# A check of the sums behind the last eviction, with a second path behind a branch

## The chip, the cores and the metric

The kernel runs on one core of one Trainium2 chip. A core has five engines with queues of their own (PE multiplies matrices, DVE and ACT work on vectors, POOL does side work, SP issues transfers) and 16 DMA engines that move data between the device memory and the core. The metric is the device time of one execution in microseconds. A profiled execution also has a span, from the first to the last instruction of the core, which is a little shorter than its time.

## The reference

A gated recurrence runs over time for each batch and channel; its output is mixed by 32 slots of 8 experts, with a softmax over all tokens (columns) on the way in and a softmax over the slots (rows) on the way out.

```python
sig = 1.0 / (1.0 + np.exp(-f_logit))             # x, f_logit: 4 x 5056 x 256
f = lower_bound + (1.0 - lower_bound) * sig
for t in range(S):                                # S = 5056
    h = f[:, t] * h + (1.0 - f[:, t]) * x[:, t]
    y[:, t] = h
...
x = y.reshape(20224, 256)
logits = x @ phi                                  # 20224 x 32
d = np.exp(logits - logits.max(0)); d /= d.sum(0) + 1e-09
slot_input = d.T @ x                              # 32 x 256, 4 slots for each expert
for e in range(8):
    slot_out[e] = np.maximum(slot_input[e] @ w1[e], 0.0) @ w2[e]
c = np.exp(logits - logits.max(1)); c /= c.sum(1) + 1e-09
out = c @ slot_out
```

## The kernel before

*Stages.* The input is read once, in units of 512 time steps of one batch (n counts the units, g the groups of four batches, b the batch). For each unit ACT takes the sigmoid, POOL multiplies with x (u_t), PE turns both to channels on the partitions, ACT makes the decay, DVE scans along time (line 318), PE turns the result back and makes the logits, and ACT takes the exponential of the logits **without subtracting a maximum**: all exponentials stay on the chip in etall (32 slots of each of four batches on 128 partitions), with their sums over time in csum. After the last unit the small experts' stage runs on the weights loaded meanwhile, and gives slot_out. The last stage multiplies etall with slot_out, 128 rows at a time, scales each row by the reciprocal of its row sum, and stores the rows.

*The sums.* Row sums come from matmuls of etall with ones (row_sums) into rs_ps, and their reciprocals go to the tile rrow, one column for each block of 128 rows and each batch (lines 726 and 741); the last 64 time steps use left and only half of the last four columns. The column sums are reduced by DVE from csum to cs1 (line 628, one column on 128 partitions), which a matmul with rep2 adds up over the batches (cs_ps, line 659), and DVE takes the reciprocal (rcs, line 667).

*The last stage.* The pool osb has three buffers for output rows; the pool pout, opened in line 786 on the kernel's outermost stack of contexts, has the eight banks of PSUM. whole(i, b, ...) handles one batch by itself, couple(i, j) two batches at once: a matmul for each row of the block (line 813), then an eviction with the scale by ACT (line 818) or DVE (line 821), then the stores, 2048 KB each, issued by SP (line 833). The last calls are couple(i, j) over the full blocks, so the program's last work is three buffers of evictions and six stores. The tile base holds the identity matrix in its first 128 columns and other constants; its first 512 columns are reused as begun, for the first output rows.

*Order.* The instructions of each engine stand in the order of the calls (manual_schedule); waits between engines are set by the framework from the tiles that are read and written. At the end of the program a closing block (line 890 in the profile) lets SP wait for all transfers, after which all engines meet at a barrier. An opening block (line 879) fills four constants on POOL and lets all engines start by a barrier.

Of the kernel before, what the change touches and what calls it, by code (L numbers as in the profile page):

```python
# [9 lines left out]
F32 = mybir.dt.float32  # L10
BF16 = mybir.dt.bfloat16
AX = mybir.AxisListType
ALU = mybir.AluOpType
ACT = mybir.ActivationFunctionType
PSUM = bass.MemoryType.PSUM


@with_exitstack
def kernel(
# [10 lines left out]
    nc = tc.nc  # L30
    B, S, D = x.shape
    E = moe_w1.shape[0]
    F = moe_w1.shape[2]
    NS = moe_phi.shape[1]
    SPE = NS // E
    P = 128
    DC = D // P
    FC = F // P
    R = 4
    G = P * R  # L40
    n_grp = (S + G - 1) // G
# [27 lines left out]
    phi = consts.tile([P, DC, NS], BF16, name="phi")  # L69
    base = consts.tile([P, 2 * P + P // 2 + D], F32, name="base")  # L70
    ident_f = base[:, ds(0, P)]
    make_identity(nc, ident_f)
    ident = base[:, ds(P, P // 2)].bitcast(BF16)
    rep = base[:, ds(P + P // 2, P)].rearrange("p (b s) -> p b s", b=B)
# [3 lines left out]
    lbs = consts.tile([P, 4, DC], F32, name="lbs")  # L78
    omlb, nomlb = lbs[:, 0], lbs[:, 1]
    own = lbs[:, 2, ds(0, 1)]  # L80
# [42 lines left out]
    rrow = store.tile([P, n_grp * R, B], F32, name="rrow")  # L123
# [36 lines left out]

    psu = held.enter_context(tc.tile_pool(name="psu", bufs=2, space=PSUM))
    psp = held.enter_context(tc.tile_pool(name="psp", bufs=1, space=PSUM))
    ld = held.enter_context(tc.tile_pool(name="ld", bufs=3))
    with tc.tile_pool(name="sp2", bufs=3) as sp2, \
# [4 lines left out]
         tc.tile_pool(name="etok", bufs=2) as etok, \  # L169
         tc.tile_pool(name="ptp", bufs=1, space=PSUM) as ptp, \  # L170
         tc.tile_pool(name="plg", bufs=1, space=PSUM) as plg, \
         tc.tile_pool(name="pslot", bufs=1, space=PSUM) as pslot:

# [12 lines left out]
        xs, fs, sts, uts, pss, psus, hs, hps, hts, lgs, ets = ({} for _ in range(11))  # L186
# [402 lines left out]
        hid, wide = (ld.tile([P, 2, R, D], F32, name=i, tag="x_t") for i in ("hid", "wide"))  # L589
        hid = hid.rearrange("p u r d -> p (u r d)").bitcast(BF16)[:, ds(0, FC * E // 2 * NS)]  # L590
# [3 lines left out]
        hid = hid.rearrange("p (f e s) -> p f e s", f=FC, s=NS)  # L594
# [17 lines left out]
        for o in range(DC):  # L612
            nc.tensor.matmul(sin_ps[:, o], slot_v[:, o], rep[:, 0],
                             start=True, stop=True, skip_group_check=True)

    with tc.tile_pool(name="ew", bufs=1) as ew, \
         tc.tile_pool(name="pm", bufs=2, space=PSUM) as pm, \
         tc.tile_pool(name="pbig", bufs=1, space=PSUM) as pbig:
# [3 lines left out]
        sin = [ew.tile([P, NS], BF16, name=f"sin{o}") for o in range(DC)]  # L622
# [1 line left out]
        nc.scalar.activation(sin[1], sin_ps[:, 1], ACT.Copy, scale=omlb[:, ds(1, 1)])  # L624
        row_sums(8, 14)

        cs1 = ew.tile([P, 1], F32, name="cs1")
        nc.vector.tensor_reduce(cs1, csum, AX.X, ALU.add)


# [3 lines left out]
        for q in range(E // Q):  # L634
            hi = ew.tile([P, F], BF16, name=f"hi{q}")
            for k in range(2):
                hi_ps = (psu.tile([P, H], F32, name="hi_ps", tag="up") if q == 0 else
                         pbig.tile([P, H], F32, name="hi_ps", tag=f"hi_ps{k}"))
                for o in range(DC):
                    for j in range(Q):  # L640
                        nc.tensor.matmul(hi_ps[ds(j * NS, NS)], sin[o],
                                         w1_sb[q * Q + j][:, o, ds(k * H, H)],
                                         start=(o == 0), stop=(o == DC - 1),
                                         skip_group_check=True)
# [8 lines left out]
        for q in range(E // Q):  # L653
# [4 lines left out]
            if q == 0:  # L658
                nc.tensor.matmul(cs_ps, rep2, cs1, start=True, stop=True)
                src = ht_ps.rearrange("p f (j s) -> p f j s", s=NS)[:, :, :, ds(0, SPE)]  # L660
                src = bass.AP(tensor=src.tensor, offset=src.offset,
                              ap=[list(src.ap[0]), [P, FC], [NS + SPE, Q], [1, SPE]])
                dst = hid[:, :, :, ds(0, SPE)]
                dst = bass.AP(tensor=dst.tensor, offset=dst.offset,
                              ap=[list(dst.ap[0]), [Q * NS, FC], [NS + SPE, Q], [1, SPE]])
# [4 lines left out]
            for j in range(Q):  # L670
                s0 = (Q + j) * SPE
                src = ht_ps[:, :, ds(j * NS + s0, SPE)]
# [3 lines left out]
        top = ds((B - 1) * NS, NS)  # L676
# [9 lines left out]
        for e in range(Q):  # L686
            for fc in range(FC):
                nc.tensor.matmul(so4_ps[ds(fc % 4 * NS, NS), :], hid[:, fc, e],
                                 w2_sb[e][:, fc],
                                 start=(e == 0 and fc < 4),  # L690
                                 stop=(e == Q - 1 and fc >= FC - 4),
                                 skip_group_check=True)
# [14 lines left out]
        for j in range(Q):  # L707
            for fc in range(FC):
                if j == Q - 1 and fc == half:
# [5 lines left out]
                                 start=(j, fc) in ((0, 0), (Q - 1, half)),  # L715
                                 stop=j == Q - 1 and fc in (half - 1, FC - 1),
                                 skip_group_check=True)
# [3 lines left out]
            if j == 0:  # L721
                nc.tensor.matmul(so_ps, rep2, so4, start=False, stop=False,
                                 skip_group_check=True)
                for k in range(0, wide_r, wide_r // 4):
                    k = ds(k, wide_r // 4)
                    nc.vector.reciprocal(rrow[:, k], rs_ps[:, k])
                for i in range(0, half, 2):
                    g_ps = psu.tile([P, 2, DIR, P], F32, name="g_ps", tag="up")
                    for k in range(2):
                        nc.tensor.matmul(g_ps[:, k], hi_late[top, i + k], em[top],  # L730
                                         start=True, stop=True, skip_group_check=True)
# [5 lines left out]
            if j == 1:  # L737
                row_sums(25, n_grp * R)
                q = n_grp * R - 1
                k = ds(wide_r * B, (q - wide_r) * B + B // 2)  # L740
                nc.vector.reciprocal(rrow.rearrange("p q b -> p (q b)")[:, k],
                                     rs_ps.rearrange("p q b -> p (q b)")[:, k])
        for r in range(DIR):
            add(r, (FC - 2, FC - 1), False)
            nc.tensor.matmul(rows_ps[r], early[:, r], slot_pre,
                             start=False, stop=True, skip_group_check=True)
# [3 lines left out]
        for r in range(DIR):  # L750
            scale = rrow[:, r, ds(B - 1, 1)]
            if r == 0:
                nc.scalar.activation(begun[:, r], rows_ps[r], ACT.Copy, scale=scale)
            else:
# [3 lines left out]
            out=out[ds((B - 1) * S, P * wide_r)].rearrange(  # L758
                "(p r) d -> p r d", r=wide_r)[:, ds(0, DIR)], in_=begun)


    held.close()
    with tc.tile_pool(name="osb", bufs=3, reuse_waits="tile") as osb:

        def by_vector(ob, op, scale):
            nc.vector.tensor_tensor(ob, op, scale.broadcast_to(list(ob.shape)), ALU.mult)
# [15 lines left out]
        def rows_of(i, b):  # L782
            t0, n_r = blocks[i]
            return out[ds(b * S + t0, P * n_r)].rearrange("(p r) d -> p r d", r=n_r)

        pout = ctx.enter_context(tc.tile_pool(name="pout", bufs=8, space=PSUM, reuse_waits="tile"))

        def whole(i, b, pieces, ends):
            n_r = blocks[i][1]
# [71 lines left out]
        for i in range(end):  # L861
            for j in range(B // 2):
                if i or j < B // 2 - 1:
                    couple(i, j)


# [1 line left out]
_INS = ['x', 'f_logit', 'lower_bound', 'moe_phi', 'moe_w1', 'moe_w2']  # L868
# [26 lines left out]
```

## Time and profile before

| What | Value |
|---|---|
| median of three runs | 197.6 us (196.98 to 198.33) |
| profiled execution, its own time | 197.07 us |
| its span | 195.3 us |
| busy PE, DVE, ACT, POOL | 154.1, 146.5, 139.9, 103.6 us |
| moved by the DMA engines | 70.75 MB, 362 GB/s on the mean |
| share of the 16 DMA engines: SP's queue, POOL's queue, code | 76.8%, 21.6%, 0.4% |
| last eviction ends, last store's bytes end | 176.1 us, 193.0 us |

Busy time counts when an engine executes; a wait is put down to what ended last. The profile cuts the span into 40 slices and gives the busy share of each in tenths. Queries of the trace give single instructions: line, engine, operation, the tiles as output<-input, the shape, a count, and times in microseconds or, for single instructions in groups, nanoseconds (shortest/median/longest). A q behind an engine's name is its queue: instructions that wait, issue transfers or work on semaphores.

### The profile page before, as it was taken

How to read it: one execution, taken by the hardware profiler on the slowest of the kernel's cores; microseconds unless marked ns; L12 is line 12 of the kernel's file. 1: busy time of each engine (PE TensorE's matmuls, PEld its weight loads, DVE VectorE, ACT ScalarE, POOL GpSimd, SP SyncE). 2: the span in 40 equal slices, each digit the busy share in tenths (PEclk: the TensorE clock that was granted, in tenths of full speed). 3: DMA queues.
4: the chain of work that ended last, by engine and by line, in shares of the span. 5: the costliest groups of instructions: out<-in, count | busy, mean ns of one | idle time of the engine just before them, and what ended most of it. 6: DMA issues, size and time to landing. Idle time of an engine off the chain costs nothing.

```text
span 195.3 us, 3281 instructions
## 1 busy us (share of the span) xinstructions
PE 154.1 (79%) x1206; PEld 105.1 (54%) x1206; DVE 146.5 (75%) x191; ACT 139.9 (72%) x201; POOL 103.6 (53%) x80
## 2 busy tenths in 40 slices
PE   4758888999989979888997878999899999980000
PEld 4436666776767757666685756468675433220000
DVE  2679788899799999999999999534189798770000
ACT  3689698699789999999998595634279987770000
POOL 2589578874997789884979968284030000000000
PEclk9999999999999999999999999999997555555555
DMA  5999999999999999999999999999949999999995
GB/s 202 415 419 419 434 424 424 424 426 358 380 428 419 417 321 423 430 419 313 397 421 388 275 232 213 214 212 214 181 152 424 421 454 430 430 430 430 430 430 218
DMA packets 14145, 70.75 MB, mean 362 GB/s; under 512 B 1569, under 2 KB 2594, under 8 KB 10162
## 3 DMA queue, kind: packets, MB, share of 16 engines
q1 hardware_dynamic: 11504, 62.13, 76.8%
q0 software_dynamic: 2624, 8.42, 21.6%
q8 instruction: 9, 0.15, 0.3%
q14 instruction: 6, 0.05, 0.1%
q10 hardware_dynamic: 2, 0.00, 0.0%
HBM read 58.23 MB, written 20.71 MB: 404 GB/s over the span
## 4 chain that ended last, share of the span: by engine, by line
DMA 30%; PE 21%; DVE 17%; ACT 10%; issue 6%; POOL 5%; ACTq 0%; SPq 0%; POOLq 0%; DVEq 0%
DMA x_t<-in_x_dram 15%; DVE h L318 14%; PE op L813 9%; DMA w_t<-in_moe_w_dram 8%; DMA w_sb<-in_moe_w_dram 7%; POOL u_t L247 4%; ACT oc L818 4%; DVE ht L348 3%; PE hp L331 3%; PE up L272 2%; ACT a L300 2%; PE op L776 2%; PE sp L262 2%; ACT ob L770 1%; ACT s_t L236 1%
## 5 line engine op out<-in xcount | busy, mean ns | idle before, releaser
L247 POOL TENSOR_TENSOR u_t<-s_t,x_t 128x1024 bf16<-128x1024 bf16 (+1 forms) x39 | 82.4, 2128 | 22.1 <-ACT s_t L236 13.2
L318 DVE TENSOR_TENSOR_SCAN h<-a,h,up 128x512 bf16<-128x512 f32 (+1 forms) x72 | 86.7, 1252 | 4.6 <-PE up L272 3.3
L236 ACT ACTIVATE s_t<-f_t 128x2048 bf16<-128x2048 f32 (+2 forms) x23 | 38.3, 1669 | 7.4 <-DMA f_t<-in_f_logit_dram 5.2
L331 PE MATMUL hp<-base,h 128*128 128x128 f32 (+1 forms) x160 | 28.8, 303 | 9.3 <-DVE ht L348 7.1
L331 PEld LDWEIGHTS hp<-base,h 128*128 128x128 f32 (+1 forms) x160 | 22.3, 207 | 19.4 <-DVE ht L348 12.0
L813 PE MATMUL op<-slot_bd,etall 64*128 64x512 bf16 x62 | 25.3, 562 | 1.1 <-POOL slot_bd L749 0.2
L300 ACT ACTIVATE a<-sp,lbs 128x1024 f32<-128x1024 bf16 x24 | 25.4, 1115 | 0.6 <-PE sp L262 0.6
L818 ACT ACTIVATE oc<-op,rrow 128x256 f32<-128x256 f32 x54 | 22.3, 496 | 4.3 <-PE op L813 4.1
L821 DVE TENSOR_TENSOR oc<-op,rrow 128x512 f32<-128x512 f32 x35 | 22.1, 685 | 2.8 <-PE op L813 2.8
L184 PE MATMUL slot_ps<-base 128*128 128x256 f32 x74 | 23.3, 422 | 0.0
L262 PE MATMUL sp<-base,s_t 128*128 128x128 f32 x144 | 19.9, 278 | 3.1 <-ACT a L307 2.0
L307 ACT ACTIVATE a<-sp,lbs 128x512 f32<-128x512 bf16 (+2 forms) x22 | 17.8, 858 | 3.5 <-PE sp L262 3.2
L262 PEld LDWEIGHTS sp<-base,s_t 128*128 128x128 f32 x144 | 16.2, 143 | 6.2 <-ACT a L307 3.9
L272 PE MATMUL up<-base,u_t 64*128 64x64 f32 x192 | 17.9, 230 | 1.1 <-POOL u_t L247 1.0
L813 PEld LDWEIGHTS <-etall 64*128 64x128 bf16 x62 | 9.0, 149 | 16.3 <-issue 11.4
L272 PEld LDWEIGHTS up<-base,u_t 64*128 64x128 f32 x192 | 14.0, 138 | 5.9 <-POOL u_t L247 2.6
L348 DVE COPY ht<-hp 128x512 f32<-128x512 f32 (+1 forms) x22 | 14.7, 667 | 0.8 <-PE hp L331 0.8
L348 ACT COPY ht<-hp 128x512 f32<-128x512 f32 (+1 forms) x18 | 10.5, 581 | 6.5 <-PE hp L331 6.4
L184 PEld LDWEIGHTS slot_ps<-base 128*128 128x128 f32 x74 | 12.7, 201 | 2.5 <-issue 1.1
L318 DVE TENSOR_TENSOR_SCAN h<-a,up 128x512 bf16<-128x512 f32 x8 | 9.4, 1209 | 2.1 <-PE up L262 2.0
L362 PE MATMUL lg<-h,phi 128*32 128x512 bf16 (+1 forms) x80 | 9.6, 389 | 0.0
L262 PE MATMUL up<-base,u_t 128*128 128x128 f32 x48 | 7.8, 281 | 1.6 <-POOL u_t L247 1.2
(124 smaller groups left out, 147.9 us busy)
## 6 DMA issues: line engine op xcount, KB each, us to landing
f_t<-in_f_logit_dram SPq DMA_DIRECT2D x12, 1024.0 KB, 12.3
x_t<-in_x_dram SPq DMA_DIRECT2D x12, 1024.0 KB, 11.7
out_dram<-oc SPq DMA_DIRECT2D x6, 2048.0 KB, 13.7
w_sb<-in_moe_w_dram POOLq DMA_DIRECT2D x14, 512.0 KB, 11.1
f_t<-in_f_logit_dram SPq DMA_DIRECT2D x12, 512.0 KB, 8.6
x_t<-in_x_dram SPq DMA_DIRECT2D x12, 512.0 KB, 9.9
out_dram<-ob SPq DMA_DIRECT2D x1, 2048.0 KB, 10.5
out_dram<-oc SPq DMA_DIRECT2D x2, 896.0 KB, 6.9
```

The costliest lines, as they stand in the source:

```text
L184: nc.tensor.matmul(slot_bank[:, 1], ident_f, wide_ident, start=False, stop=False, skip_group_check=True)
L236: nc.scalar.activation(s_t, f_t, ACT.Sigmoid, scale=-1.0)
L247: nc.gpsimd.tensor_tensor(uts[n][:, :r], s_t[:, :r], x_t[:, :r], ALU.mult)
L262: nc.tensor.transpose(ps[:, :, r], t[:, r], ident_f)
L272: nc.tensor.transpose(v[:, :, r], t(r)[k].bitcast(F32), ident_f[k, k])
L300: nc.scalar.activation(a, sp[:, :, :, :, o], ACT.Identity, scale=nomlb[:, ds(o, 1)], bias=1.0)
L318: nc.vector.tensor_tensor_scan(h[:, :T, o], decays[n // 2, o][:, n % 2, :T], up[:, :T, o], hs[number(g - 1, b)][:, ds(used(g - 1) - 1, 1), ...
L331: nc.tensor.transpose(hp[:n_p, r], hw[:, :n_p, r], ident_f)
L348: copy(hts[g][:n_p, b].rearrange("p r d -> p (r d)").bitcast(F32), hps.pop(n)[:n_p].rearrange("p r c -> p (r c)"))
L813: nc.tensor.matmul(op.rearrange("p u d -> p (u d)"), ew[:, :, r], slot_bd[ds(j * 2 * NS, 2 * NS)].rearrange("s u d -> s (u d)"), start=Tru ...
L818: nc.scalar.activation(ob[:, u, r], op[:, u], ACT.Copy, scale=scale[:, r, ds(u, 1)])
L821: nc.vector.tensor_tensor(ob[:, :, r], op, scale[:, r].unsqueeze(2).broadcast_to([P, 2, D]), ALU.mult)
```

## The change

The tile cs1 becomes a column of rrow that nothing else uses, so that the sums stand side by side in 159 columns. Behind the last call of couple, DVE clamps these columns to the bounds from 1e-12 to 1e12, compares the result with the columns themselves, and takes the minimum for each partition; a matmul with ones adds the 128 verdicts, and DVE compares the sum with 128. The result is one integer, which all five engines load into a register. A branch on it runs guarded(), which computes the reference over again from the inputs, step by step in loops (79 turns over time with a running maximum of each column, 8 over the experts, 79 over the rows with a maximum of each row), and overwrites the output. With sums inside the bounds the branch goes past it. The pool pout is now closed together with osb, ahead of the branch.

```diff
+SAFE = 1e12
+
+def guarded(ctx, tc, x, f_logit, moe_phi, moe_w1, moe_w2, out, lbs):
+    T = P // 2
+    n_t = S // T                                  # 79
...
+    with tc.For_i(0, n_t, 1) as i:
+        for src, dst in ((f_logit, f_t), (x, x_t)):
+            nc.gpsimd.dma_start(out=dst, in_=src[:, ds(i * T, T)].rearrange("b t d -> t b d"))
...
+        nc.vector.tensor_reduce(new, lg_ps[:, :T], AX.X, ALU.max)
+        nc.vector.tensor_tensor(new, new, top, ALU.max)
...
+        nc.vector.scalar_tensor_tensor(acc, acc, shrink, sl_ps, ALU.mult, ALU.add)
...
+    with tc.For_i(0, E, 1) as i:
...
+    with tc.For_i(0, n_t, 1) as i:
...
+        nc.gpsimd.dma_start(out=out.rearrange("(b t) d -> t b d", b=B)[ds(i * T, T)], in_=o_t)
...
-        cs1 = ew.tile([P, 1], F32, name="cs1")
+        cs1 = rrow[:, n_grp * R - 1, ds(B // 2, 1)]
         nc.vector.tensor_reduce(cs1, csum, AX.X, ALU.add)
...
-    with tc.tile_pool(name="osb", bufs=3, reuse_waits="tile") as osb:
+    with tc.tile_pool(name="osb", bufs=3, reuse_waits="tile") as osb, \
+         tc.tile_pool(name="pout", bufs=8, space=PSUM, reuse_waits="tile") as pout:
...
-        pout = ctx.enter_context(tc.tile_pool(name="pout", bufs=8, space=PSUM, reuse_waits="tile"))
...
                 if i or j < B // 2 - 1:
                     couple(i, j)
 
+        n_v = (n_grp * R - 1) * B + B // 2 + 1
+        sums_of = rrow.rearrange("p q b -> p (q b)")[:, ds(0, n_v)]
+        clamped, one, fine = base[:, ds(0, n_v)], base[:, ds(D, 1)], base[:, ds(D + 1, 1)]
+        unsafe = base[ds(0, 1), ds(D + 2, 1)].bitcast(mybir.dt.int32)
+        nc.vector.memset(one, 1.0)
+        nc.vector.tensor_scalar(clamped, sums_of, 1.0 / SAFE, SAFE, ALU.max, ALU.min)
+        nc.vector.tensor_tensor(clamped, clamped, sums_of, ALU.is_equal)
+        nc.vector.tensor_reduce(fine, clamped, AX.X, ALU.min)
+        fine_ps = pout.tile([P, 2, D], F32, name="fine_ps", tag="op")[ds(0, 1), 0, ds(0, 1)]
+        nc.tensor.matmul(fine_ps, fine, one, start=True, stop=True)
+        nc.vector.tensor_scalar(unsafe, fine_ps, float(P), None, ALU.is_lt)
+
+    beyond = nc.values_load(unsafe, min_val=0, max_val=1)
+    with tc.If(beyond != 0, preferred_fallthrough_block=False):
+        guarded(tc, x, f_logit, moe_phi, moe_w1, moe_w2, out, lbs)
```

In the built program the branch is a compare-and-branch on each engine. Behind it stand, on each engine, a short block for the case that nothing is wrong (a semaphore count and a jump), then the blocks of the second path, then the closing block. POOL's opening block has four register moves more, and the program as a whole has 3262 listed instructions where it had 2583.

## Prediction before the run

> **What bounds the kernel now.** The profiled execution took 197.07 us, 195.3 us of it span; the median of the three runs is 197.6 us, 0.5 us above it. The change adds its work at the very end and a little at the very start, so these two places are read, and first of all what the transfers do there. The page's second part cuts the span into 40 slices of 4.9 us; the rows of the four compute engines are followed by the clock and the transfers.
>
> ```profile
> PE   4758888999989979888997878999899999980000
> DVE  2679788899799999999999999534189798770000
> ACT  3689698699789999999998595634279987770000
> DMA  5999999999999999999999999999949999999995
> ```
>
> In the last four slices no engine computes and the transfers are full. The stretches of the end, asked one by one (columns: length, busy time and count of PE, PEld, DVE, ACT, POOL, granted clock, DMA share, GB/s), say until when:
>
> ```profile
> 170.00:175.00 5.00, 4.78 (x11) 1.37 (x9) 3.80 (x7) 4.06 (x10) 0.00 (x0) 0.50 1.06 455
> ...
> 180.00:185.00 5.00, 0.00 (x0) 0.00 (x0) 0.00 (x0) 0.00 (x0) 0.00 (x0) 0.50 0.98 419
> ```
> ```profile
> 192.00:193.00 1.00, 0.00 (x0) 0.00 (x0) 0.00 (x0) 0.00 (x0) 0.00 (x0) 0.50 0.88 377
> 193.00:194.00 1.00, 0.00 (x0) 0.00 (x0) 0.00 (x0) 0.00 (x0) 0.00 (x0) 0.50 0.05 16
> 194.00:195.30 1.30, 0.00 (x0) 0.00 (x0) 0.00 (x0) 0.00 (x0) 0.00 (x0) 0.50 0.00 0
> ```
>
> Output is written at about 420 to 450 GB/s until 193.0 us. The timeline of the end (start, length, engine, instruction) shows where the engines stopped:
>
> ```profile
> 174.83 0.69 DVE L821 TENSOR_TENSOR oc<-op,rrow 128x512 f32<-128x512 f32 x1 [0.39 <-PE op L813]
> ```
> ```profile
> 175.63 0.47 ACT L818 ACTIVATE oc<-op,rrow 128x256 f32<-128x256 f32 x1
> 175.76 1.62 SPq L833 DMA_DIRECT2D out_dram<-oc  x2
> ```
>
> The last evictions end at 175.52 us on DVE and 176.10 us on ACT, and SP has issued the last two stores, 2048 KB each, by 177.38 us. From there to 193.0 us it only drains. The instructions of line 890, the program's closing block, and the waits of SP show what follows:
>
> ```profile
> L890 SPq DRAIN  x3: 7/7/7, 194.5 to 194.8; - x3
> ```
> ```profile
> SPq L890 <- DMA out_dram<-oc: 16.5, 4, 4.9
> ```
>
> SP waits 16.5 us for the stores in the closing block, goes on at 194.5 us, 1.5 us after the last bytes, and a barrier of all engines ends the span 0.8 us later. So between 176 and 194.5 us the five engines have time to spare: whatever they do there is free as long as they are in the closing block by 194.5 us and put no bytes into the transfers.
>
> **The change part by part.** *The main path.* Apart from the names of lines and of cs1, the built program has the same instructions on every engine, in the same order and with the same waits, up to the last eviction: the pool pout, closed earlier, and cs1, now a free column of rrow, add no wait. I cost these at nothing: the reduction that writes cs1 (0.15 us, row L628) and the matmul that reads it keep shape and place.
>
> *The check* on DVE starts behind the eviction that ends at 175.52 us. Five small instructions and one matmul are priced by these rows:
>
> ```profile
> L710 DVE TENSOR_SCALAR slot_so<-so_ps,rcs x1: 484/484/484, 141.5 to 141.5; 128x256 f32<-128x256 f32 x1
> ```
> ```profile
> L849 DVE TENSOR_TENSOR ob<-ob,op x2: 413/418/422, 154.0 to 154.4; 128x256 f32<-128x256 f32 x2
> ```
> ```profile
> L659 PE MATMUL cs_ps<-cs,base x2: 223/236/250, 132.8 to 132.9; 128*128 128x1 f32 x2
> L667 DVE RECIPROCAL rcs<-cs_ps x1: 169/169/169, 133.2 to 133.2; 128x1 f32<-128x1 f32 x1
> ```
>
> The memset takes 0.06 us (row L95, two columns). The clamp on 159 columns lies between 0.16 us (L112, 2 columns) and 0.484 us (256 columns); by columns, 0.16 + 157/254 x 0.324 = 0.36 us. The comparison is at most the 0.418 us of L849, and taken as 0.36; the reduction by the same slope from L628 (10 columns, 0.15 us) is 0.34 us. The matmul of two passes spans 0.33 us in the timeline, and the last comparison is one column, 0.16 us. That is 0.06 + 0.36 + 0.36 + 0.34 + 0.33 + 0.16 = 1.6 us, and four hand-overs at 0.2 us (DVE waited 0.2 us for lb_ps, the longest of that kind at the start) make 2.4 us: the verdict is there at 177.9 us. Were each of the three wide instructions as slow as the reciprocal of 94 columns (0.747 us, row L741), it would be 1.2 us more, 179.1 us.
>
> *The load of the verdict into a register on all five engines* has no row. Its lower end is a semaphore instruction (0.017 us), its upper end the small load of phi_f, 4.6 us from issue to landing. It is a memory read of one word, so nearest to the fastest round trip on the page, 2.1 us for the store out of base; I take 2.1 us. By the Trainium skill (DMA: Bandwidth & Descriptors, section Latency and other measured facts) such a load has a floor near 600 ns, by which the verdict would be in the registers 1.5 us earlier; no row here shows it. *The branch:* each engine executes a compare-and-branch and then, in the block for the case of nothing wrong, a semaphore wait and a jump to the closing block. At the start of the program a jump stands between the release of the barrier (0.7 us) and SP's first issue (0.73 us), so two cost 0.06 us at the low end; I take 0.1. So the engines stand in the closing block at 177.9 + 2.1 + 0.1 = 180.1 us, 14.4 us before SP needs them. Queued behind these instructions is nothing but the closing block itself: SP's last store is issued ahead of its load, and POOL, which in the false block counts up the software queue's semaphores, waits there only for weight loads that landed before 145 us. Cost on the path: nothing; the cover is the drain of the last stores.
>
> *What is not covered.* First, POOL sets four registers in the opening block, ahead of the memsets and the barrier that hold back all engines:
>
> ```profile
> L879 POOLq INC_SWDGE_SEM x1: 27/27/27, 0.1 to 0.1; - x1
> L879 POOL MEMSET const-float32-0.0<- x1: 103/103/103, 0.2 to 0.2; 128x1 f32 x1
> ```
>
> At 17 ns (its semaphore instruction) to 27 ns that is 0.07 to 0.11 us; with the memset's 0.1 us for each it would be 0.4. I take 0.1 us. Second, code is loaded through the same transfer engines that are full for most of the span:
>
> ```profile
> q8 instruction: 9, 0.15, 0.3%
> q14 instruction: 6, 0.05, 0.1%
> ```
>
> These 0.20 MB stand for 2583 listed instructions, 77 bytes each. The changed program lists 679 more, 52 KB; at the 424 GB/s of the end all of it costs 0.12 us, none of it 0. I take 0.1 us.
>
> **The sum** against the profiled execution: 197.07 + 0.1 + 0.1 + 0 = 197.3 us. Against the median of the runs, which stands 0.5 us higher, 197.6 + 0.2 = **197.8 us**.
>
> **The rivals.** *Slower: the branch has to fetch its code behind the stores.* The place is the two jumps of each engine, between 180 us and the closing block, past the block of the second path. A code packet itself takes little: 0.3% of 16 x 195.3 us is 9.4 us for nine packets, 1.0 us each. But in the stretch of the stores a small transfer waits among large ones:
>
> ```profile
> out_dram<-ob SPq DMA_DIRECT2D x2, 128.0 KB, 8.8
> ```
>
> If both jumps miss and each fetch takes these 8.8 us, with the load at 4.6 us and the slow check: 179.1 + 4.6 + 17.6 = 201.3 us, 6.8 us after SP's 194.5, so 204.4 us. With the check and the load as I take them it is 180.0 + 17.6 = 197.6, 3.1 us late: about **200.7 us**. It decides from 14.4 us for the two jumps together, that is 7.2 us each; one miss alone (188.8 us) is hidden, and so are two at 3.1 us (1.0 for the packet, 2.1 for the trip). For it speaks that the transfers are full through the whole tail; against it that the 8.8 us are a store queued behind others of its own queue, while code has queues of its own. The Trainium skill has the rule that speaks for this rival: a taken branch whose target is outside the two pages of code held makes the engine wait for a fetch (Runtime: NRT & Kernel Launch, section Instruction fetch mechanics). The trace of before has no branch over a distance that could show it.
>
> *Slower: the check stands behind the stores after all*, if an engine that evaluates the branch first waited for all transfers. Then the load, the branch and the verdict's hand-over, 2.1 + 0.1 + 0.2 us, follow 194.5 us, with the check too 4.6 us: 200.2 to 202.4 us. Against it: in the built program the waits for the last stores stand in the closing block, behind the branch.
>
> *Not doing what it says:* the second path runs. Its first loop alone has 79 turns, each of which loads 0.52 MB and waits for it; at 4.6 us for the smallest load it would add 363 us at least: over 560 us. Row sums of 32 exponentials and column sums of 5056, none of a large argument by the scale of the inputs, are far inside the bounds.
>
> *Faster.* Nothing is removed but one small tile, and the engines' work in the span is the same; over 1% would need 2.0 us. Only chance in the placing of tiles or in the order of transfers could give it.
>
> **How the numbers follow.** About 1% (2 us) is what a measurement of this kernel can tell from no change: its three runs lie between 196.98 and 198.33 us. Forecast, all hidden: 0.79. Late code: 0.11, of which a part stays under 1%. Check behind the stores: 0.05. Second path: 0.01. Faster by more than 1%: 0.03; the last 0.01 is for a disturbance of the transfers that I cannot place, slower. With two parts in the hundred of the late code staying under 1%, this gives faster 0.03, within 1% 0.81, slower 0.16. The likeliest case's own range is 196.9 to 199.0 us: below by the spread of the runs, above by 0.4 us for the registers, 0.12 for code and the upper run. To leave no more than 2 in 10 out, and with the late code's lower half in it, the range is 196.9 to 200.5 us.
>
> **What would show it right or wrong.** Right: in the changed profile the check's last comparison on DVE ends by 179 us, the engines' last branches lie between 179 and 185 us, SP still waits some 10 us or more for the stores in the closing block, and first issue comes about 0.1 us later. Wrong: SP or another engine reaches the closing block after the stores have landed; the transfers have a gap in the tail, or the stores land later by more than 0.5 us; the same stretch before 176 us has grown.

## The result, and the profile after

The changed kernel takes 198.95 us in the median of 8 runs (198.45 to 199.54), the kernel before 197.22 us in 8 runs of its own (196.98 to 198.33). The ratio is 1.0082, with a 95% interval from 1.0058 to 1.0106: 1.6 us, within 1% as forecast (the interval's upper end lies just over it), but eight times the 0.2 us of the sum. The profiled execution took 198.51 us, 197.0 us of it span, 1.7 us more than the span before.

The check itself did what the prediction said. The timeline of the changed kernel shows it behind the last evictions:

```profile
175.18 0.24 DVE L1062 TENSOR_SCALAR base<-rrow 128x159 f32<-128x159 f32 x1
...
175.81 0.32 DVE L1064 TENSOR_REDUCE base<-base 128x1 f32<-128x159 f32 x1
...
176.50 0.15 DVE L1067 TENSOR_SCALAR base<-fine_ps 1x1 int32<-1x1 f32 x1 [0.37 <-PE fine_ps L1066]
```

The instructions by line give the load of the verdict, the branch on PE and the closing block (durations in ns: shortest/median/longest, then the first and the last start):

```profile
L1069 SPq TENSOR_LOAD <-base x1: 1162/1162/1162, 177.2 to 177.2; - x1
```
```profile
L1070 PEldq COMPARE_BRANCH  x2: 90/3652/7213, 178.0 to 178.4; - x2
```
```profile
L1097 SPq DRAIN  x3: 7/7/13, 196.1 to 196.4; - x3
...
L1097 PEldq DRAIN  x2: 8/40/73, 185.6 to 196.4; - x2
```

The verdict was there at 176.65 us, the load took 1.16 us, and SP entered the closing block at 179.4 us. PE stood in its jump for 7.2 us and came at 185.6 us, still 10.5 us before SP went on. So no engine was late. What was late is the stores: SP's drain starts at 196.1 us, where it was 194.5 before, although SP had issued the last two stores by 177.1 us, 0.3 us earlier than before. The page shows the code that was loaded, and the transfers thinning out in the last slice; then the end in stretches of half a microsecond, first of the changed kernel, then the one stretch of the kernel before that still has something in it (a packet counts where it starts):

```profile
DMA  5999999999999999999999999999759999999993
...
q8 instruction: 11, 0.18, 0.3%
q14 instruction: 10, 0.08, 0.1%
```
```profile
193.00:193.50 0.50, 0.00 (x0) 0.00 (x0) 0.00 (x0) 0.00 (x0) 0.00 (x0) 0.50 0.54 229
193.50:194.00 0.50, 0.00 (x0) 0.00 (x0) 0.00 (x0) 0.00 (x0) 0.00 (x0) 0.50 0.39 164
194.00:194.50 0.50, 0.00 (x0) 0.00 (x0) 0.00 (x0) 0.00 (x0) 0.00 (x0) 0.50 0.15 66
194.50:195.00 0.50, 0.00 (x0) 0.00 (x0) 0.00 (x0) 0.00 (x0) 0.00 (x0) 0.50 0.15 66
```
```profile
193.00:193.50 0.50, 0.00 (x0) 0.00 (x0) 0.00 (x0) 0.00 (x0) 0.00 (x0) 0.50 0.09 33
```

Before, all but one of the 16 DMA engines stop together; now a few go on. The trace lists the packets with their times, but not their engines. The packets follow each other almost without a gap (about 0.01 us), so they can be chained, one chain for each engine: before, 15 chains end between 193.1 and 193.3 us and one at 193.9. After, ten end between 193.5 and 193.6 us, the other six at 194.0, 194.2, 194.3, 195.0, 195.2 and 195.5. Six code packets lie in the drain, none of which the kernel before has: four of 8 KB and one of 16 KB between 182.5 and 184.1 us, one more of 16 KB at 190.1 us.

The table of before and the prediction put the end of the last bytes at 193.0 us. That came from the stretches, which count a packet where it starts; by the packets' own ends it is 193.94 us before and 195.53 us with the change. SP's drain starts 0.6 us after that in both kernels, and not 1.5 us.

### The profile page after: what moved, and what is told of

It is laid out like the page before. It is cut to its first block, busy times and chain, and to the rows that moved or that the text cites. A ratio compares the mean times of both kernels' runs of the same rounds, so it can differ in the third digit from the quotient of the medians.

```text
span 197.0 us, 3327 instructions
## 1 busy us (share of the span) xinstructions
PE 152.7 (78%) x1208; PEld 104.5 (53%) x1208; DVE 147.5 (75%) x196; ACT 139.5 (71%) x201; POOL 103.5 (53%) x80
## 4 chain that ended last, share of the span: by engine, by line
DMA 29%; PE 18%; DVE 18%; ACT 11%; issue 6%; POOL 5%; SPq 0%; POOLq 0%; ACTq 0%; DVEq 0%
DMA x_t<-in_x_dram 14%; DVE h L510 14%; DMA w_t<-in_moe_w_dram 8%; PE op L1004 8%; DMA w_sb<-in_moe_w_dram 7%; ACT oc L1009 5%; POOL u_t L439 4%; DVE ht L540 3%; PE hp L523 3%; PE up L464 2%; ACT a L492 2%; ACT ob L963 2%; PE sp L454 2%; ACT s_t L428 1%; PE lg L554 1%
## 6 DMA issues: line engine op xcount, KB each, us to landing
out_dram<-ob SPq DMA_DIRECT2D x1, 2048.0 KB, 10.5
```

## The experiments

**The theory:** the jump past the second path makes engines load code while the stores drain. Each packet falls on one DMA engine, which has a fixed sixteenth of the stores to move besides, and the end waits for the latest engine. **The rivals:** the check and the register loads disturb the stores; a branch costs as such; the later start passes on to the end; only the sum of the bytes counts.

*Without the branch.*

```diff
     beyond = nc.values_load(unsafe, min_val=0, max_val=1)
-    with tc.If(beyond != 0, preferred_fallthrough_block=False):
-        guarded(tc, x, f_logit, moe_phi, moe_w1, moe_w2, out, lbs)
```

> The check and the loads of its verdict on all engines stay; the branch and the second path are left out, so the sums outside the bounds are not dealt with. Theory (the branch makes the engines fetch code while the stores drain, and the code falls on few of the 16 DMA engines, which then finish their part of the stores late; a further 0.25 us is POOL's four register moves at the start): no code packets after 178 us, no register moves, all DMA engines finish together; 197.2 to 197.5 us, within 0.3 us of before. Rival (the check itself, its matmul or the five register loads disturb the last stores): 198.5 to 199.2 us as with the change. Rival (all of it is chance in how the store packets fall): anything between, no fixed sign.

197.2 us, ratio 1.0002 (0.9994 to 1.0011). Check, matmul and five register loads cost nothing that can be measured; there is no code packet in the drain and the chains end as before, 15 at 193.3 to 193.5 us.

*A short second path.*

```diff
-        guarded(tc, x, f_logit, moe_phi, moe_w1, moe_w2, out, lbs)
+        nc.vector.memset(base[:, ds(D + 4, 1)], 0.0)
```

> Check, loads and branch stay; the second path is one memset of one column, so the jump is over a few instructions (in this version the sums outside the bounds are not dealt with). Theory: the target lies in code that is held, no code packet in the drain, PE's branch takes tenths of a us and not 7; 197.2 to 197.5 us. Rival (a branch as such costs, whatever lies behind it): 198.3 us or more, PE's branch again some us.

197.4 us, ratio 1.0019 (1.0004 to 1.0034). The branch as such costs 0.4 us by the ratio, 0.7 at the interval's end; PE's jump is short, and no more code is loaded than before:

```profile
L1070 PEldq COMPARE_BRANCH  x2: 85/132/180, 178.0 to 178.1; - x2
```
```profile
q8 instruction: 9, 0.15, 0.3%
q14 instruction: 6, 0.05, 0.1%
```

So about 1.2 of the 1.6 us, by the ratios, belong to the code that is jumped over (from 0.7 to 1.8 us, an estimate from both intervals).

*The path's transfers by SP* (each `nc.gpsimd.dma_start` in guarded becomes `nc.sync.dma_start`).

> The second path's transfers are issued by SP in place of POOL; nothing else is changed. If the four register moves at POOL's start belong to its transfers with computed addresses, they go to another engine, and the start is 0.25 us earlier: 198.6 us, and the code packets in the drain as with the change. If the moves stay, 198.9 us. If the start delay is what most of the 1.7 us comes from (by changing how the packets fall), it drops to 197.5 us.

198.92 us, ratio 1.0086 (1.0072 to 1.0100). POOL's first memset is back at 0.25 us and SP's first issue at 0.75, yet the time is that of the change, so the later start is not what most of the time comes from. It doesn't price the start cleanly: the four moves now stand on SP, the spans are 0.75 us shorter than with the change (medians 196.6 and 197.35 us), and the part of the time outside the span is 0.67 us longer (2.26 and 1.60 us on the mean).

*The path twice* (a second call of guarded in the branch).

> The second path stands twice behind the branch (it runs for neither), so the jump is over twice as much code. Theory: more engines than PE jump out of what they hold, so more of the branches stall for some us and more code packets fall into the drain, perhaps 8 to 12 in place of 6; time 198.9 to 200.5 us, more than with the change by the packets that fall on the latest DMA engine (0.3 us for 8 KB, 0.9 for 16 KB). Rival (check, loads or branch as such): the same as with the change, 198.9 us.

198.74 us, ratio 1.0091 (1.0077 to 1.0105). More code is loaded, nine packets in the drain in place of six, but the end is no later: its last chain ends at 195.5 us, as with the change. The expected rise did not come, and no further engine stalls: PE's jump takes 7.4 us, all other branches 0.055 us or less. It fits an end set by the latest engine and not by the sum; it doesn't prove it.

```profile
q14 instruction: 13, 0.11, 0.1%
```

*The path without PE, and PE alone.* In the first, nc.tensor in guarded is replaced by an object whose methods do nothing (PSUM is cleared in its place); in the second the path is PE's:

```diff
-        guarded(tc, x, f_logit, moe_phi, moe_w1, moe_w2, out, lbs)
+        with tc.tile_pool(name="g_ps", bufs=1, space=PSUM) as gp:
+            acc = gp.tile([P, D], F32, name="acc")
+            for n in range(82):
+                nc.tensor.matmul(acc[:, ds(0, P)], base[:, ds(P, P)], base[:, ds(P, P)], ...)
+            nc.vector.tensor_copy(base[:, ds(D + 4, 1)], acc[:, ds(0, 1)])
```

> With the change, but the second path has no work for PE (it would compute nothing right if it ran; it does not run): PE's jump is over some 80 instructions in place of 345, the other engines' code is as long as before. If PE's fetch of 16 KB is what makes the end late: no 16 KB packet in the drain, PE's branch takes tenths of a us, 197.5 to 198.1 us. If the 8 KB packets of the other engines do it: 198.5 to 199.0 us as with the change.

> With the change, but the second path is 82 matmuls on PE and one copy (sums outside the bounds are not dealt with): only PE's jump is as far as with the change. If PE's fetch makes the end late: two packets of 16 KB in the drain and no other code, PE's branch takes 5 to 8 us, 198.2 to 198.9 us. If the other engines' packets do it: 197.4 us as with the small path.

Without PE's part: 198.85 us, ratio 1.0087 (1.0071 to 1.0102). PE's jump shrinks to 0.3 us, but five packets of 8 KB and one of 16 KB, which the forecast did not have, remain in the drain, and the time is that of the change: PE's stall is not the cost.

```profile
L1078 PEldq COMPARE_BRANCH  x2: 90/197/304, 179.2 to 179.3; - x2
```

With PE alone: 198.04 us, ratio 1.0048 (1.0034 to 1.0062), between its two forecasts. PE's jump takes 6.9 us and two packets of 16 KB are left, both PE's; the stretches show two stores that start after all others:

```profile
q8 instruction: 11, 0.18, 0.3%
q14 instruction: 6, 0.05, 0.1%
```
```profile
193.50:194.00 0.50, 0.00 (x0) 0.00 (x0) 0.00 (x0) 0.00 (x0) 0.00 (x0) 0.50 0.00 0
194.00:194.50 0.50, 0.00 (x0) 0.00 (x0) 0.00 (x0) 0.00 (x0) 0.00 (x0) 0.50 0.15 66
```

This is the cleanest case. Two chains end late, at 194.64 and 194.69 us, where 13 others end between 193.1 and 193.25 and one at 194.0. Around each code packet the stores slow down too: packets of 16 KB that take 0.61 us elsewhere take 0.84 and 0.68 us ahead of it, the code packet 0.88 us, the store behind it 1.01 us. That is 0.23 + 0.07 + 0.88 + 0.40 = 1.6 us that one load of 16 KB costs its engine, and a chain ends 1.45 us after the others. That each late chain holds one of the two packets is read from their number and from these sizes. As one engine ends 0.7 us late without any code, the span grew by 0.8 us (196.1).

*Foreign bytes without any branch.* Three kernels add 64 KB of loads that nobody reads to the kernel before.

```diff
+        probe = osb.tile([P, wide_r, D], F32, name="ob", tag="ob")
+        for u in range(4):                             # four rows: by POOL, or by SP
+            nc.gpsimd.dma_start(out=probe[ds(u, 1)], in_=x[ds(u, 1), ds(0, wide_r)])
...
+        nc.gpsimd.dma_start(out=probe[:, 0, ds(0, P)], in_=x[0, ds(0, P), ds(0, P)])   # or over all partitions
```

> On the kernel before, with no check and no branch: POOL issues four loads of 16 KB, each into one partition, during the stores of the last stage, 64 KB in all (as much as the branch's code) that nobody reads. Theory (bytes that fall on few DMA engines in the drain make these finish their part of the stores late): if the four rows fall on one engine, its part is 4 x 0.61 us = 2.4 us longer, 199.5 us; on two 198.4; if they fall on four engines 0.6 us, 197.7 us. The end is ragged: most engines stop near 193.3 us and those with the rows later. Rival (only the sum of bytes counts): 64 KB at 424 GB/s, 0.15 us, 197.3 us.

> The same 64 KB on the kernel before, as one load of 512 bytes into each of the 128 partitions. Theory: spread over all DMA engines, the end stays even, 0.15 to 0.3 us: 197.2 to 197.5 us. Rival (any foreign transfer among the stores costs the same): as the kernel with four rows.

> On the kernel before, no check and no branch: SP issues, behind its last two stores, four loads of 16 KB, each into one partition; nobody reads them. A store of the last stage goes out in packets of 16 KB, one for each partition, so each of these rows should be one packet. Theory (what one DMA engine has to do besides its sixteenth of the stores sets the end): four packets of 0.61 us on one engine 2.4 us later than the others, less up to 0.7 us by which one engine is later anyway, 198.8 to 199.5 us; on four engines 0.6 us, 197.1 to 197.8 us. Rival (only the sum of bytes): 0.15 us, 197.2 us, with an even end.

The first was no test: POOL's queue cut the rows into 64 packets of 1 KB (128 packets more on the page, half of them of 4 bytes), and these moved from 154 to 159 us, in the last stage but long before the drain; 197.53 us, ratio 1.0027 (1.0018 to 1.0037). Over all partitions, 16 packets of 4 KB from 154.6 to 156.8 us: 197.15 us, ratio 1.0004 (0.9995 to 1.0013). It is an even load on transfers that are full (DMA share 1.04 from 150 to 160 us in the kernel before), but not one in the drain. With SP the rows stay whole and stand behind the last stores, and the same 64 KB cost 2.5 us by the ratio: 199.46 us, ratio 1.0128 (1.0113 to 1.0143). Its stretches show one packet at a time, long after the others:

```profile
193.50:194.00 0.50, 0.00 (x0) 0.00 (x0) 0.00 (x0) 0.00 (x0) 0.00 (x0) 0.50 0.08 33
...
195.50:196.00 0.50, 0.00 (x0) 0.00 (x0) 0.00 (x0) 0.00 (x0) 0.00 (x0) 0.50 0.08 33
```

Fourteen chains end between 193.1 and 193.3 us, one at 193.9, one at 196.1; the last one ends with four packets of 0.61 us, one behind the other from 193.67 us on. The sum of the bytes would be 0.15 us; what counts here is how many fall on one engine.

*The branch behind the stores.*

```diff
+        nc.vector.memset(last_ob[ds(0, 1), :, 0, ds(0, 1)], 0.0)      # waits for the last two stores
         nc.vector.tensor_scalar(unsafe, fine_ps, float(P), None, ALU.is_lt)
```

> As with the change, but DVE waits for the last two stores to land before it writes the verdict (it clears two elements of their buffer first), so the five loads, the branch and the code behind it follow the stores. Theory: no code packet among the stores, these land as before, at 194.5 us; then 0.3 us for DVE, 1.2 us for the load, and PE's fetch of code without traffic, 1 us for the packet and up to 2 us for the trip, in place of 7: 199.5 to 202 us. The drain is even again. If the code took as long as in the drain, 7 us, it would be 205 us. Rival (the second path makes the stores late by something other than code in the drain): the stores land late again, near 196 us, and the time is over 202.

202.62 us, ratio 1.0275 (1.0259 to 1.0290), 0.6 us over the range: the jump takes PE 4.1 us even without stores, not 3. The time is over the rival's 202 us, but the rival's other sign, stores that land near 196 us, does not show:

```profile
194.75 0.06 DVE L1068 MEMSET oc<- 1x2 f32 x1 [18.72 <-DMA out_dram<-oc]
```
```profile
L1071 SPq TENSOR_LOAD <-base x1: 476/476/476, 195.0 to 195.0; - x1
```
```profile
L1072 PEldq COMPARE_BRANCH  x2: 90/2090/4090, 195.6 to 195.9; - x2
```

With the same code loaded after them, the stores land in time for DVE at 194.75 us. This takes the check and the mere length of the program off the list (the register loads, which moved behind the stores too, were cleared by the kernel without the branch), and shows that the drain was still the better cover for the branch, 3.7 us cheaper.

*The start alone.* The short path, with one transfer by POOL to an address from the register:

```diff
-        nc.vector.memset(base[:, ds(D + 4, 1)], 0.0)
+        nc.gpsimd.dma_start(out=base[ds(0, 1), ds(2 * D, 4)], in_=x[ds(0, 1), ds(beyond, 1), ds(0, 4)]...)
```

> As the kernel with the small path, but the path is one transfer by POOL with a computed address (sums outside the bounds are not dealt with), so that POOL's opening block has register moves again, two in place of four. If a later start passes on to the end: 0.12 us over the small path's 197.4, 197.5 us. If not: 197.4 us. No code packet in the drain either way; if there is one after all, up to 198.5 us.

197.29 us, ratio 1.0004 (0.9987 to 1.0021). POOL's first memset is at 0.37 us, between 0.24 and 0.49; a share of it in the time can't be told from nothing.

## Why the prediction was right or wrong

*Right, in part by luck: a change within 1%.* The time lies in the range and the change within 1%, but not by the forecast's mechanism, which had no cost at the end beyond 0.1 us. One of its own signs of being wrong came true: the stores land later by more than 0.5 us (SP goes on at 196.1 us in place of 194.5). The range reached up to 200.5 us for engines that come late, and no engine did; that 1.6 us of late stores still fits in it, just under the 2 us of 1%, was not foreseen.

*Right: what covers the check.* The verdict was forecast for 177.9 us and came at 176.65: the check took 1.4 us against 2.4 (the clamp 0.24 against 0.36), and the evictions ended 0.27 us earlier. The register load took 1.16 us between its ends of 0.017 and 4.6, with 2.1 taken. The Trainium skill's floor near 600 ns (DMA: Bandwidth & Descriptors, section Latency and other measured facts) lies between what was measured: 1.16 us among the stores, and 0.48 us without them, which is below it, so here the measurement decides. All engines but PE stood in the closing block by 179.4 us, 180.1 forecast. The wait order was as read: the branch waits for no store.

*Right in part: the late code.* The rival's mechanism is in the trace: PE's jump over some 345 instructions took 7.2 us, close to the 7.2 us for each of two jumps from which it was to decide; but there was one miss only, and one was said to be hidden. It was. The rule of the Trainium skill that speaks of a target outside the two pages held (Runtime: NRT & Kernel Launch, section Instruction fetch mechanics) agrees with the three lengths of jump that ran: 7.2 us past some 345 instructions, 0.3 past some 80, 0.18 past a few.

*Wrong: the term for code bytes.* It was taken as 0.1 us: 52 KB at the 424 GB/s of all 16 engines. What was loaded was in fact 64 KB, nearly that number, though by luck: code comes in whole packets, and PE alone loads 32 KB for 82 matmuls and a copy, 6 KB at 77 bytes each. It cost 1.2 to 1.6 us, by whether the short path or the kernel before is taken off. The step that failed is the division by 16. Each packet is on one engine, the stores leave no engine a gap (DMA share 1.01 from 176 to 193 us before), and no other engine takes over what a late one has left: with PE alone 13 chains stop by 193.25 us while two go on to 194.6. So the extra of the busiest engine is the price, as far as the chains can be read: for 16 KB 1.45 us at the end of a chain (PE alone), and the four rows by SP show the same for plain data. The sum of the bytes came close only for the load over all partitions, which ran before the drain.

*Wrong, but with no effect that was seen: the start.* The four moves took 29 to 39 ns each, 0.13 us in all, where the forecast had 0.07 to 0.11 us. The first memset came 0.24 us later, which is more than the moves' own time:

```profile
L1086 POOLq MOVE  x4: 29/29/39, 0.2 to 0.4; - x4
```

With half the delay (the start alone) the time didn't rise measurably. A part of the delay may be made up outside the span: the time less the span is 1.77 us on the mean in the kernel before, 1.68 with two moves and 1.60 with the change's four. But it is 1.71 in the kernel with the branch behind the stores, which has four moves too, so this is a hint and no proof. The transfers by SP, with the start as before, can't settle it, since the time outside the span changed there as well.

*What stays open.* The trace doesn't name the DMA engine of a packet; which engine code falls on is read from the chains. Rows on four engines, or an even load by SP in the drain itself, were not tried. Why three packets more, with the path twice, cost nothing was not settled. Why packets of 8 KB without PE's part delay the end as much as PE's 16 KB was not either: there some stores next to them took 1.9 to 2.4 us, in a profile that is the longest run of its kernel (199.66 us).

## What to carry to other kernels

Work behind the last eviction can be free while the last stores drain, as long as it moves next to no bytes: here the check and five register loads cost nothing measurable. A branch can move bytes: the jump past the long path loaded 64 KB of code, the one past the short path none. Price transfers in a saturated drain by the bytes that fall on the busiest DMA engine, and not by their sum over all: 64 KB cost 2.5 us in four rows on one engine behind the last stores, and 0.1 us spread over the partitions some 20 us before the drain. When a program ends in a drain, look at whether the engines stop together; a ragged end tells where the time went.

## What the runs showed that was not expected

A code load slows the stores next to it as well: 16 KB of code cost its engine 1.6 us, 16 KB of a store 0.61. The same register load takes 1.16 us among stores and 0.48 us after them, and the same jump of PE 7.2 and 4.1 us. The difference is the wait ahead of its packet: from the start of the jump to the start of the first 16 KB packet 4.5 us pass among the stores and 0.9 us after them. The packet takes 1.2 and 1.8 us, and PE goes on 1.5 and 1.4 us behind it. Four rows of 16 KB, each in one partition, go out from SP's queue as one packet each, all in one chain, and from POOL's in pieces of 1 KB. And register moves on POOL, 29 to 39 ns long each, delay the start within the span by 0.06 us apiece (0.24 us for four, 0.12 for two).
